# Gated linear attention feeding four experts: a state of two heads in 96 columns, and the additions and splits around it moved

## The chip, the cores and the metric

The kernel runs on one core of a Trainium2 chip. The metric is device time in microseconds (us) for one execution of the whole program. The core has a matrix engine (TensorE, called PE in the profile, with its weight loads listed apart as PEld), a vector engine (VectorE, DVE), a scalar engine (ScalarE, ACT), GpSimd (POOL) and a sync engine (SP) whose queue issues most of the transfers. Each engine works through its own instruction queue in order. Matrix products land in PSUM; everything else lives in SBUF or in device memory.

## The reference

Two blocks follow each other. The first is a gated linear attention over 4 batches, 8 heads, 768 positions and 48 features, with a state of 48x48 for each head:

```
state = alpha[:, :, t, :, None] * state + einsum('bhd,bhe->bhde', k[:, :, t], v[:, :, t])
y[:, :, t] = einsum('bhd,bhde->bhe', q[:, :, t], state)
```

Its result is laid out as 3072 rows of 384 (8 heads x 48). The second block sends every row through four experts and adds the results, weighted by normalised probabilities:

```
p = domain_probs / (domain_probs.sum(-1, keepdims=True) + 1e-09)
for e in range(4):
    h = np.maximum(x @ w1[e], 0.0)          # w1[e]: 384 x 1024
    out += p[:, e:e + 1] * (h @ w2[e])      # w2[e]: 1024 x 384
```

All is float32 on the outside.

## The kernel before

**Units and groups.** The 3072 rows are 24 units of 128 rows: 6 blocks of positions (`cb`) of each of 4 batches (`b`). The units are put in 7 groups: two units in the first (group 0) and the last (group 6), four in each of the five between. While the experts work on one group, the attention of the next group is woven in. `deal` makes a plan for that: each attention is a generator with some 17 steps, each step has a due time on a clock of estimated costs, and `advance` runs the steps that are due each time the expert loops add their estimated cost to the clock. What the plan yields is a fixed order of instructions for each engine.

**Experts.** For each group and each of the 4 experts there is an "up" stage (`up`, x @ w1, 8 column tiles of 128) and a "down" stage (`down`, h @ w2). From group 1 on, the up products are made from three parts of each float32 number: x is split into `top` (a rounded copy, made by ACT), `low` and `dif` (made by DVE, lines 242 and 243), and three fast float32r products (line 500) are summed, two parts into the PSUM tile `one`, the third into `two`. In groups 2 to 5 the down stage is made so too (line 576, `split2`). There the down stage goes over the four units in two turns of two ("pairs" below). A pair has 48 matmuls of 128x384: steps 0 to 23 are parts 0 and 1 of both units for the first six of the eight row tiles of h, steps 24 to 31 are the same parts for the last two row tiles (28 and 29 end part 1 of the first unit, 30 and 31 of the second), steps 32 to 39 are part 2 of the first unit, steps 40 to 47 part 2 of the second. Parts 0 and 1 are summed in the tile `ops0` of a unit, part 2 in `ops1`.

**Additions.** `add_up` (line 598) adds one such sum, scaled, to the unit's accumulator `acc`. In the kernel before, a unit's fine sum (`ops0`, scaled by `p_fine`) is added as soon as its part 1 is done, that is after step 29 for the first unit and after step 31 for the second; the other sum (`ops1`, scaled by `p_all`) after steps 39 and 47. With expert 0 the fine addition is a copy on ACT (line 607); all others are on DVE (line 609).

**The four banks.** `one`, `two`, `ops0` and `ops1` share four PSUM banks under the tag "g". A new tile takes the bank that comes free first in the program's order, and its first matmul waits until the last reader of the tile before is done. So the first matmul of the next pair, or of the next up stage, waits for the first fine addition of the pair before it.

**The second halves of `dif`.** The part `dif` of h is made by DVE in halves (line 542). The second halves are kept in a list, `later`, and one is issued at every fifth step of the down stages (steps 4, 9, 14, ..., 34, 39, 44).

**The next group's x.** `split_x` (line 450) makes the three parts of x for the next group during the last expert's down stage. In the kernel before, its step 0 makes `top` for all three column blocks of x in three ACT instructions (line 456) at the start of that stage; its steps 1 to 3 make `low` and `dif` of one column block each with two DVE instructions (lines 242 and 243), at 0.52, 0.62 and 0.72 of the stage. In groups 2 to 4 the two DVE instructions of a block have 128x512 elements, in group 5 128x256 (the last group has two units only).

**Attention.** Within a unit, scores are formed in seven levels of halving (lines 295 to 341); then line 415 makes the unit's output `yps` in three blocks `c` of 128 columns of PSUM partitions. Two heads make a pair `p`, four pairs in all. A head's 48 features are cut in 32 (`QUAD`) and 16 (`TAIL`): blocks 0 and 1 hold the first 32 features of four heads each, block 2 the last 16 of all eight heads. Four matmuls with 32 output columns each, side by side in the array, are a "turn" in this document. A turn reads either the state (`past`, against QT) or the values of this block of positions (against `lat`). The state `st` has 64 columns for a head: `sts` is 128 x 4 pairs x 2 heads x 64. In a pair the second head's last features lie in columns 48 to 63 and the first head's in columns 32 to 47, so that block 2 takes two turns on the state, one for each head of the pairs, and two on the values. After the output, line 436 makes keys^T with values for the pair in 128 columns (`sps`), and lines 442 to 445 decay the state and add to it (DVE, 64 partitions x 256 elements). That happens in 20 of the 24 units; 20 units read a state.

Of the kernel before, what the change touches and what calls it, by code (L numbers as in the profile page):

```python
# [20 lines left out]
def kernel(  # L21
# [37 lines left out]
    nc = tc.nc  # L59
# [45 lines left out]
    sts = [const.tile([P, NP, 2, HD], F32, name=f"st{b}") for b in range(B)]  # L105
# [48 lines left out]
    def load(u, names):  # L154
        if u >= len(units):
            return
        cb, b = units[u]
        for nm in names:
            src = srcs[nm][b, :, cb * P:(cb + 1) * P, :].rearrange("h s d -> s h d")
            if nm != "v":  # L160
                nc.sync.dma_start(out=raw(u, nm)[:, :, :D], in_=src)
                continue

            pairs = raw(u, nm).rearrange("p (a i) d -> p a i d", i=2)
            src = src.rearrange("p (a i) d -> p a i d", i=2)
            nc.sync.dma_start(out=pairs[:, :, 0, :D], in_=src[:, :, 0])
            nc.sync.dma_start(out=pairs[:, :, 1, :QUAD], in_=src[:, :, 1, :QUAD])
            nc.sync.dma_start(out=pairs[:, :, 1, D:], in_=src[:, :, 1, QUAD:])
# [70 lines left out]
    def split_rest(x, out):  # L239

        top, low, dif = out
        nc.vector.tensor_sub(low, x, top.bitcast(F32))  # L242
        nc.vector.scalar_tensor_tensor(out=dif, in0=top.bitcast(F32), scalar=1 / 4096.0,
                                       in1=low.bitcast(F32), op0=ALU.mult, op1=ALU.subtract)
# [18 lines left out]
    def attention(u):  # L263
# [140 lines left out]
        st = sts[b]  # L404
        yps = ps.tile([P, KC, P], F32, name="yps", tag="w")
        for c in range(KC):

            if c < 2:
                turns = [[(j, 2 * c + j // 2, j % 2, slice(0, QUAD)) for j in range(4)]]
            else:  # L410
                turns = [[(p, p, i, slice(QUAD, HD)) for p in range(NP)] for i in range(2)]
            terms = [(t, past) for past in ((True, False) if cb > 0 else (False,)) for t in turns]
            for n, (turn, past) in enumerate(terms):
                for j, p, i, cols in turn:
                    nc.tensor.matmul(  # L415
                        yps[QUAD * j:QUAD * (j + 1), c, :],
                        lhsT=st[:, p, i, cols] if past else rv[:, 2 * p + i, cols],
                        rhs=QT[:, p, :] if past else lat[:, 2 * p + i, :],
                        start=(n == 0), stop=(n == len(terms) - 1))
# [10 lines left out]
        if cb < NCB - 1:  # L430
            KB = AT
            nc.scalar.copy(out=KB, in_=turned(lambda p: KT[:, p, :]))
            yield
            sps = ps.tile([P, NP, 2, HD], F32, name="sps", tag="w")
            for p in range(NP):
                nc.tensor.matmul(sps[:, p], lhsT=KB[:, p, :], rhs=rv[:, 2 * p:2 * p + 2, :],  # L436
                                 start=True, stop=True)
            for i in range(2):
                rows = slice(HD * i, HD * (i + 1))
                old, add = st[rows, :, i, :], sps[rows, :, i, :]  # L440
                if cb == 0:
                    nc.vector.tensor_copy(out=old, in_=add)
                else:
                    nc.vector.tensor_mul(old, old, decs[-1][rows].broadcast_to([HD, NP, HD]))
                    nc.vector.tensor_add(old, old, add)
# [4 lines left out]
    def split_x(gi, step):  # L450

        n = len(groups[gi]) * P
        if step == 0:
            xTs[gi] = work.tile([P, 3, KC, NT], F32R, name="xT", bufs=1)
            for kc in range(KC):
                nc.scalar.activation(out=xTs[gi][:, 0, kc, :n], in_=xraws[gi][:, kc, :n],
                                     func=ACT.Copy, scale=TRIM)
        else:
            kc = step - 1
            split_rest(xraws[gi][:, kc, :n], [xTs[gi][:, part, kc, :n] for part in range(3)])  # L460
# [88 lines left out]
    def down(gi, e, slots, between):  # L549
# [14 lines left out]
        for n, (part, i, fc) in enumerate(steps):  # L564
# [17 lines left out]
            if part >= 1 and fc == FCH - 1:  # L582
                add_up(gi, e, slots[i], part // 2, sums[i][part // 2 if halves_ else 0])
        while between:
            between.popleft()[1]()
# [12 lines left out]
    def add_up(gi, e, slot, kind, part):  # L598

        cb, b = groups[gi][slot]  # L600
        at = b * NCB + cb
        if e == 0 and (kind == 0 or not split2(gi, e)):
            accs[cb, b] = hid.tile([P, DM], F32, name="acc", bufs=B)
        acc = accs[cb, b]
        scale = (p_fine if kind == 0 else p_all)[:, at, e:e + 1]
        if e == 0 and (kind == 0 or not split2(gi, e)):
            nc.scalar.activation(out=acc, in_=part, func=ACT.Copy, scale=scale)
        else:
            nc.vector.scalar_tensor_tensor(out=acc, in0=part, scalar=scale, in1=acc,  # L609
                                           op0=ALU.mult, op1=ALU.add)  # L610
        if kind == 0:
            return
# [50 lines left out]
    with tc.manual_schedule():  # L663
# [48 lines left out]
        for gi, e in ((gi, e) for gi in range(len(groups)) for e in range(E)):  # L712
# [6 lines left out]
            for k, slots in enumerate(turns):  # L719

                between = deque()
                if e == E - 1 and gi + 1 < len(groups):
                    for step, at in enumerate((0.0, 0.52, 0.62, 0.72)):
                        at = at * len(turns) - k
                        if 0 <= at < 1:
                            between.append((at, lambda step=step: split_x(gi + 1, step)))
# [33 lines left out]
```

## Time and profile before

| | |
|---|---|
| three runs | 1087.1 us median (1086.73 to 1088.61) |
| the profiled execution's own time | 1087.1 us |
| span of the profile in it | 1085.3 us |
| PE busy, PEld busy | 1062.9 us (98%), 892.9 us (82%) |
| DVE busy | 747.7 us (69%) |
| ACT busy | 560.7 us (52%) |
| POOL busy | 35.3 us (3%) |

The span is the profiled part of the execution; 1.8 us lie around it. In the page's 40 slices PE is at nine tenths or more from the sixth slice to the last but one. DVE is at six to eight tenths in most of them, and at one tenth in the last three. The first expert matmul (line 492) starts at 26.4 us, and the first one of group 1 (line 500) at 170.6 us. A line of a timeline merges instructions of one kind that follow each other: the first number is the start in us from the span's start, the second how long they took together, "x4" that they are four; brackets say how long the engine was idle before and what ended it. The last instruction's end can overlap the next one's start by some hundredths of a microsecond.

### The profile page before, as it was taken

The numbers are of one execution on the slowest core, as the hardware profiler recorded it, in microseconds if no ns is written. First come the engines' busy times: TensorE is split into PE (matmuls) and PEld (weight loads), VectorE is DVE, ScalarE is ACT, GpSimd is POOL, SyncE is SP. The second block draws the span as 40 slices with busy tenths as digits, with TensorE's granted clock in tenths as the row PEclk, the third lists the DMA queues.
The fourth block names the chain that finished last, engine by engine and source line by source line (L and its number), as shares of the span: only waits on it lengthen the run. The fifth ranks groups of instructions, "written<-read, shape, count | busy, mean of one in ns | idle before, by whom it ended". The sixth has DMA issues, their size and how long they took to land.

```text
span 1085.3 us, 21700 instructions
## 1 busy us (share of the span) xinstructions
PE 1062.9 (98%) x8532; PEld 892.9 (82%) x8532; DVE 747.7 (69%) x1625; ACT 560.7 (52%) x1191; POOL 35.3 (3%) x75
## 2 busy tenths in 40 slices
PE   8889899999999999999999999999999999999998
PEld 8767677686776798898898898898988998899876
DVE  5588678647557869778878787986786876757111
ACT  5787776674646555545546445555454454222321
POOL 2000000000000100000000000000000000000000
PEclk9999999999999999999999999999999999999999
DMA  8597789786696967657759559477477568545982
GB/s 124 154 327 216 228 266 370 290 312 234 211 322 218 400 203 275 273 169 301 254 171 358 201 190 357 158 276 306 151 291 287 201 259 349 235 197 238 309 312 91
DMA packets 166197, 273.68 MB, mean 252 GB/s; under 512 B 120624, under 2 KB 140976, under 8 KB 142032
## 3 DMA queue, kind: packets, MB, share of 16 engines
q1 hardware_dynamic: 156704, 230.06, 61.0%
q0 software_dynamic: 6016, 42.08, 9.9%
q8 instruction: 67, 1.10, 0.4%
q10 hardware_dynamic: 3376, 0.17, 0.3%
q14 instruction: 34, 0.28, 0.1%
HBM read 229.81 MB, written 42.47 MB: 251 GB/s over the span
## 4 chain that ended last, share of the span: by engine, by line
PE 87%; ACT 5%; DVE 5%; issue 2%; POOL 0%; ACTq 0%; DVEq 0%; POOLq 0%
PE ops L576 24%; PE one L500 21%; PE ops L580 13%; PE two L500 10%; PE sc L328 6%; PE yps L415 4%; PE one L492 3%; PE tp L260 3%; ACT qb L302 2%; PE sps L436 1%; PE far L383 1%; PE idle L689 1%; DVE near L338 1%; DVE hT L534 1%; DVE t L509 1%
## 5 line engine op out<-in xcount | busy, mean ns | idle before, releaser
L576 PE MATMUL ops<-w,hT 128*128 128x384 f32 x1536 | 284.7, 340 | 2.1 <-DVE acc L609 2.1
L500 PE MATMUL one<-xT,w 128*128 128x512 f32 (+1 forms) x1104 | 275.3, 385 | 0.8 <-DVE xT L242 0.8
L576 PEld LDWEIGHTS ops<-w,hT 128*128 128x128 f32 x1536 | 265.9, 188 | 5.7 <-DVE acc L609 2.8
L500 PEld LDWEIGHTS one<-xT,w 128*128 128x128 f32 x1104 | 194.5, 188 | 43.4 <-issue 2.6
L507 ACT ACTIVATE t<-one 128x512 f32<-128x512 f32 (+1 forms) x184 | 103.1, 560 | 149.4 <-PE one L500 148.8
L580 PE MATMUL ops<-hT 128*128 128x384 f32 x512 | 176.1, 491 | 0.0
L302 ACT COPY qb<-QT 64x256 f32<-64x256 f32 x336 | 136.5, 406 | 70.1 <-DVE QT L283 40.2
L500 PE MATMUL two<-xT,w 128*128 128x512 f32 (+1 forms) x552 | 148.3, 377 | 0.0
L580 PEld LDWEIGHTS ops<-hT 128*128 128x128 f32 x512 | 94.0, 191 | 56.5 <-issue 1.3
L534 DVE SCALAR_TENSOR_TENSOR hT<-t,hT 128x512 fp32r<-128x512 f32 x128 | 88.7, 693 | 61.1 <-ACT hT L532 59.7
L532 ACT ACTIVATE hT<-t 128x512 fp32r<-128x512 f32 x128 | 80.9, 632 | 95.8 <-DVE t L509 94.6
L500 PEld LDWEIGHTS two<-xT,w 128*128 128x128 f32 x552 | 100.3, 188 | 19.8
L542 DVE SCALAR_TENSOR_TENSOR hT<-hT 128x256 fp32r<-128x256 f32 x256 | 101.3, 421 | 4.4
L509 DVE TENSOR_TENSOR t<-t,two 128x512 f32<-128x512 f32 x128 | 87.3, 682 | 20.6 <-PE two L500 12.6
L609 DVE SCALAR_TENSOR_TENSOR acc<-ops,p_all,acc 128x384 f32<-128x384 f32 x88 | 53.3, 612 | 58.6 <-PE ops L580 42.3
L338 DVE COPY_PREDICATED near<-masks,sc 128x256 f32<-128x256 uint8 x144 | 77.0, 535 | 17.6 <-PE sc L328 14.5
L309 DVE TENSOR_TENSOR QT<-QT,dec 128x256 f32<-128x256 f32 x144 | 60.7, 421 | 32.5 <-ACT qb L302 32.0
L328 PEld LDWEIGHTS sc<-qb,KT 128*64 128x64 f32 x2304 | 72.5, 138 | 8.9 <-issue 6.3
L512 DVE TENSOR_TENSOR hT<-t,two 128x512 f32<-128x512 f32 (+1 forms) x56 | 32.1, 574 | 65.8 <-ACT t L507 56.1
L328 PE MATMUL sc<-qb,KT 128*64 128x64 f32 x2304 | 76.7, 223 | 0.3 <-ACT qb L302 0.3
L321 DVE TENSOR_TENSOR KT<-KT,dec 128x256 f32<-128x256 f32 x144 | 60.1, 417 | 2.2 <-PE tp L260 2.2
L320 ACT COPY KT<-KT 128x256 f32<-128x256 f32 x144 | 59.8, 415 | 3.1
(79 smaller groups left out, 927.0 us busy)
## 6 DMA issues: line engine op xcount, KB each, us to landing
w<-kept SPq DMA_DIRECT2D x156, 1152.0 KB
kept<-w POOLq DMA_DIRECT2D x32, 1152.0 KB, 7.5
hT<-in_moe_w_dram SPq DMA_DIRECT2D x48, 384.0 KB
w<-in_moe_w_dram SPq DMA_DIRECT2D x60, 128.0 KB
ra<-in_alpha_dram SPq DMA_DIRECT2D x23, 192.0 KB
rk<-in_k_dram SPq DMA_DIRECT2D x23, 192.0 KB
rq<-in_q_dram SPq DMA_DIRECT2D x23, 192.0 KB
out_dram<-acc POOLq DMA_DIRECT2D x22, 192.0 KB, 5.8
```

The source lines that it names most:

```text
L302: nc.scalar.copy(out=qb[rows, :, i, :].rearrange("p a (b r) -> p a b r", r=m), in_=qv[rows])
L309: nc.vector.tensor_mul(qv, qv, spread(dv[:, :, :, 0], m))
L328: nc.tensor.matmul(out[HALF * s:HALF * (s + 1), 2 * p:2 * p + 2, :], lhsT=KTs[li][:, p, HALF * s:HALF * (s + 1)], rhs=qbs[li][:, p, :, QUA ...
L338: nc.vector.copy_predicated(near.rearrange("p a (b two r) -> p a b two r", two=2, r=m)[:, :, :, 1, :], mk.unsqueeze(1).broadcast_to([P, H, ...
L500: nc.tensor.matmul(out, lhsT=w[:, part, kc], rhs=xTs[gi][:, part, kc, :n], start=(part == terms[0] and kc == 0), stop=(part == terms[-1] a ...
L507: nc.scalar.activation(out=t, in_=one, func=ACT.Copy, scale=FINE)
L509: nc.vector.tensor_add(t, t, two)
L532: nc.scalar.activation(out=top, in_=x, func=ACT.Relu, scale=TRIM)
L534: nc.vector.scalar_tensor_tensor(out=low, in0=x, scalar=0.0, in1=top.bitcast(F32), op0=ALU.max, op1=ALU.subtract)
L542: nc.vector.scalar_tensor_tensor(out=dif, in0=top.bitcast(F32), scalar=1 / 4096.0, in1=low.bitcast(F32), op0=ALU.mult, op1=ALU.subtract)
L576: nc.tensor.matmul(sums[i][part // 2], lhsT=h[:, part], rhs=w, start=(fc == 0 and part != 1), stop=(fc == FCH - 1 and part != 0))
L580: nc.tensor.matmul(sums[i][0], lhsT=h[:, 2].bitcast(F32), rhs=w, start=(fc == 0), stop=(fc == FCH - 1))
```

## The change

Three things change together.

- **The state and what is read of it.** The state of a pair of heads takes 96 columns in place of 128: first head's 32 features, first head's last 16, second head's last 16, second head's 32. The last features of both heads lie side by side in columns 32 to 63, and block 2 reads them in one turn. `sps` has 96 columns, and the DVE instructions of the state have 64 x 192 elements. The values are laid out to match: of the second head the last 16 features come first. The values themselves keep 64 columns for a head, with zeros behind the features, and block 2 still takes two turns on them.
- **The additions of a down stage.** A unit's two sums are added together after its part 2: `ops0` and then `ops1` of the first unit after step 39, of the second after step 47.
- **The split of the next group's x.** One column block at a time, `top` on ACT and then `low` and `dif` on DVE, at 0.25, 0.5 and 0.75 of the last expert's down stage. With two pairs this is step 24 of the first pair, step 0 of the second and step 24 of the second.

```
-    sts = [const.tile([P, NP, 2, HD], F32, name=f"st{b}") for b in range(B)]
+    sts = [const.tile([P, NP, 2, D], F32, name=f"st{b}") for b in range(B)]
...
-            nc.sync.dma_start(out=pairs[:, :, 1, :QUAD], in_=src[:, :, 1, :QUAD])
-            nc.sync.dma_start(out=pairs[:, :, 1, D:], in_=src[:, :, 1, QUAD:])
+            nc.sync.dma_start(out=pairs[:, :, 1, :TAIL], in_=src[:, :, 1, QUAD:])
+            nc.sync.dma_start(out=pairs[:, :, 1, TAIL:D], in_=src[:, :, 1, :QUAD])
...
-    def split_rest(x, out):
+    def split(x, out):
         top, low, dif = out
+        nc.scalar.activation(out=top, in_=x, func=ACT.Copy, scale=TRIM)
         nc.vector.tensor_sub(low, x, top.bitcast(F32))
...
+        flat_st = st.rearrange("p a i d -> p a (i d)")
+        flat_v = rv.rearrange("p (a i) d -> p a (i d)", i=2)
...
             if c < 2:
-                turns = [[(j, 2 * c + j // 2, j % 2, slice(0, QUAD)) for j in range(4)]]
+                now = [[(2 * c + j // 2, j % 2, (0, HD + TAIL)[j % 2], 2 * QUAD * (j % 2))
+                        for j in range(4)]]
+                turns = ([(True, now[0])] if cb > 0 else []) + [(False, now[0])]
             else:
-                turns = [[(p, p, i, slice(QUAD, HD)) for p in range(NP)] for i in range(2)]
-            terms = [(t, past) for past in ((True, False) if cb > 0 else (False,)) for t in turns]
+                turns = [(True, [(p, 0, 0, QUAD) for p in range(NP)])] if cb > 0 else []
+                turns += [(False, [(p, i, QUAD + TAIL * i, 0) for p in range(NP)]) for i in range(2)]
...
-            sps = ps.tile([P, NP, 2, HD], F32, name="sps", tag="w")
+            sps = ps.tile([P, NP, 2, D], F32, name="sps", tag="w")
             for p in range(NP):
-                nc.tensor.matmul(sps[:, p], lhsT=KB[:, p, :], rhs=rv[:, 2 * p:2 * p + 2, :],
+                nc.tensor.matmul(sps[:, p], lhsT=KB[:, p, :], rhs=rv[:, 2 * p:2 * p + 2, :D],
                                  start=True, stop=True)
...
-    def split_x(gi, step):
+    def split_x(gi, which):
         n = len(groups[gi]) * P
-        if step == 0:
+        if 0 in which:
             xTs[gi] = work.tile([P, 3, KC, NT], F32R, name="xT", bufs=1)
-            for kc in range(KC):
-                nc.scalar.activation(out=xTs[gi][:, 0, kc, :n], in_=xraws[gi][:, kc, :n],
-                                     func=ACT.Copy, scale=TRIM)
-        else:
-            kc = step - 1
-            split_rest(xraws[gi][:, kc, :n], [xTs[gi][:, part, kc, :n] for part in range(3)])
+        for kc in which:
+            split(xraws[gi][:, kc, :n], [xTs[gi][:, part, kc, :n] for part in range(3)])
...
-            if part >= 1 and fc == FCH - 1:
-                add_up(gi, e, slots[i], part // 2, sums[i][part // 2 if halves_ else 0])
-        while between:
-            between.popleft()[1]()
+            if part >= 2 and fc == FCH - 1:
+                add_up(gi, e, slots[i], sums[i])
         background()
...
+        scales = (p_fine, p_all) if split2(gi, e) else (p_all,)
+        if e == 0:
             accs[cb, b] = hid.tile([P, DM], F32, name="acc", bufs=B)
         acc = accs[cb, b]
+        for j, (part, scale) in enumerate(zip(sums, scales)):
+            if e == 0 and j == 0:
+                nc.scalar.activation(out=acc, in_=part, func=ACT.Copy, scale=scale[:, at, e:e + 1])
+            else:
+                nc.vector.scalar_tensor_tensor(out=acc, in0=part, scalar=scale[:, at, e:e + 1],
+                                               in1=acc, op0=ALU.mult, op1=ALU.add)
...
-                    for step, at in enumerate((0.0, 0.52, 0.62, 0.72)):
-                        at = at * len(turns) - k
+                    for kc in range(KC):
+                        at = (kc + 1) / (KC + 1) * len(turns) - k
                         if 0 <= at < 1:
-                            between.append((at, lambda step=step: split_x(gi + 1, step)))
+                            between.append((at, lambda kc=kc: split_x(gi + 1, [kc])))
```

## The prediction

> **What bounds the kernel now.** I read the page's busy times and chain of waits, then the groups of instructions with shapes kept apart, then the timelines of DVE and PE at the ends of the down pairs.
>
> ```profile
> PE 1062.9 (98%) x8532; PEld 892.9 (82%) x8532; DVE 747.7 (69%) x1625; ACT 560.7 (52%) x1191; POOL 35.3 (3%) x75
> PE 87%; ACT 5%; DVE 5%; issue 2%; POOL 0%; ACTq 0%; DVEq 0%; POOLq 0%
> ```
>
> PE is the chain: PE work that goes after the first 142 us is gained, and a wait that PE gets is lost. Prices are in the groups (busy us, mean ns | idle before); a float32 matmul has two records, a float32r one has one:
>
> ```profile
> L576 PE MATMUL ops<-w,hT 128*128 128x384 f32 x1536 | 284.7, 340 | 2.1 <-DVE acc L609 2.1
> L436 PE MATMUL sps<-rv,AT 128*128 128x128 f32 x160 | 21.3, 276 | 1.3 <-ACT AT L432 1.3
> L436 PEld LDWEIGHTS sps<-rv,AT 128*128 128x128 f32 x160 | 20.7, 191 | 3.9 <-ACT AT L432 1.8
> L415 PEld LDWEIGHTS yps<-QT,st 128*32 128x32 f32 x640 | 17.5, 111 | 7.3 <-issue 6.5 <-ACT hT L532 0.7
> ```
>
> PE waits for an addition in only two places of line 576, 2.1 us in all. Both end the first pair of a last expert. This is DVE around the first, then PE there and at the second (start, duration, instruction):
>
> ```profile
> 514.42 1.42 DVE L542 SCALAR_TENSOR_TENSOR hT<-hT 128x256 fp32r<-128x256 f32 x4
> 515.76 1.13 DVE L609 SCALAR_TENSOR_TENSOR acc<-ops,p_fine,acc 128x384 f32<-128x384 f32 x2
> 516.81 0.41 DVE L309 TENSOR_TENSOR QT<-QT,dec 128x256 f32<-128x256 f32 x1
> 517.14 0.16 DVE L311 TENSOR_TENSOR dec<-dec 128x8 f32<-128x8 f32 x1
> 517.22 0.42 DVE L321 TENSOR_TENSOR KT<-KT,dec 128x256 f32<-128x256 f32 x1
> 517.56 0.75 DVE L542 SCALAR_TENSOR_TENSOR hT<-hT 128x256 fp32r<-128x256 f32 x2
> 518.23 0.61 DVE L609 SCALAR_TENSOR_TENSOR acc<-ops,p_all,acc 128x384 f32<-128x384 f32 x1
> ...
> 520.33 0.68 DVE L242 TENSOR_TENSOR xT<-x_raw,xT 128x512 fp32r<-128x512 f32 x1
> 521.04 0.69 DVE L243 SCALAR_TENSOR_TENSOR xT<-xT 128x512 fp32r<-128x512 f32 x1
> ```
>
> ```profile
> 514.19 1.12 PE L576 MATMUL ops<-w,hT 128*128 128x384 f32 x5
> 516.42 0.78 PE L576 MATMUL ops<-w,hT 128*128 128x384 f32 x3 [1.11 <-DVE acc L609]
> 686.15 1.13 PE L576 MATMUL ops<-w,hT 128*128 128x384 f32 x5 [1.01 <-DVE acc L609]
> ```
>
> The pair's matmuls are spaced 0.17 us, so it ends at 515.14. DVE is behind by then: it reaches the first fine addition only at 515.76, ends it at 516.36, and PE goes on at 516.42. PE's delay is 1.28 us (the bracket counts less, since the last matmul's tail overlaps it).
>
> **State read in one turn.** It takes one of four turns of block 2 from 20 units. In PE's timeline two such turns start at 362.82 and the next work at 363.26, so a turn is 0.22 us: 20 x 0.22 = **4.4 us gained**. PE is the bound in every unit that reads a state.
>
> **sps in 96 columns.** 21.3 us over 20 units is 1.065 us for eight records; with the last one's 276 ns that leaves 113 ns from one to the next. If the step goes with the columns, 96 take 85 ns: 160 x 28 ns = 4.5 us. But each record loads 128 columns of weights, and loads take 191 ns for 128 columns and 111 for 32: 0.83 ns a column, 107 ns for 128. Then only 6 ns x 160 = 1.0 us can go, and perhaps nothing. No row with 128-column weights here is spaced closer than 109 ns, so I take the load: **0.5 us gained**, ends 0 and 4.5. A loss has no reason: nothing is added.
>
> The Trainium skill, page "TensorE: Matmul & The Clock Gate", section "LDWEIGHTS (loading the stationary operand)", has a load take its columns divided by 1.2, in ns; by it 128 columns are 107 ns, and narrowing the moving side buys next to nothing. Going by the matmul row alone the total below would be 4 us lower, by the rule it stands.
>
> **State instructions of DVE.** 72 instructions of 64x256 become 64x192. 256 elements take 419 ns (line 445) and 512 take 682 (line 509), so 64 fewer save 66 ns, 4.7 us of DVE in all. Nearly all falls where DVE catches up anyway, before it waits 0.7 us for the last relu of an up stage (line 532); I count 0.2 us, ends 0 and 1.
>
> **Values.** Transfers, bytes and queue order stay as they were, but for two pieces of 32 and 16 features that swap; no wait in the list of waits is for them. Nothing. GpSimd zeroes less before the first transposes: nothing.
>
> **Additions later.** Each first fine addition moves from step 29 to step 39 on DVE, behind everything issued between: two halves of `dif` (steps 34 and 39), what attention has there, and in a last expert the first split of x (step 24). The next pair's first matmul waits for that addition. Its seventh takes the bank of the first unit's other sum, whose addition follows 0.53 us behind; the seventh comes 1.04 us after the first, so it waits for nothing more. For the place shown (515.1), the changed program's DVE order puts these ahead of the fine addition: the QT, dec and KT row (516.81 to 517.56, 0.75), the two halves (517.56 to 518.23, 0.67) and one split (520.33 to 521.65, 1.32): **2.74 us**. PE already waits for it, so all of it is lost: the delay grows from 1.28 to 4.02. The same at 685.0: another 2.74. The other pair ends, where DVE has slack or not (start of the fine addition against the pair's end, plus what is put ahead of it, plus 0.61 for itself and 0.06 to PE):
>
> ```profile
> 848.07 0.75 DVE L542 SCALAR_TENSOR_TENSOR hT<-hT 128x256 fp32r<-128x256 f32 x2
> 848.74 1.13 DVE L609 SCALAR_TENSOR_TENSOR acc<-ops,p_fine,acc 128x384 f32<-128x384 f32 x2
> 849.79 0.75 DVE L542 SCALAR_TENSOR_TENSOR hT<-hT 128x256 fp32r<-128x256 f32 x2
> 850.46 1.13 DVE L609 SCALAR_TENSOR_TENSOR acc<-ops,p_all,acc 128x384 f32<-128x384 f32 x2
> ```
>
> This pair ends at 849.47, so -0.73 + 0.67 (halves) + 1.32 (split) + 0.67 = 1.92 us of new wait. At 601.4 and 771.1: -0.79 + 1.07 (two halves, QT, dec) + 0.67 = 0.95, less 0.09 waited today: 0.86 each. At 642.5: -1.04 + 0.67 + 0.67 = 0.30. At 925.7: -0.78 + 0.67 + 0.67 = 0.56. At 996.1, where the split has 256 columns: -1.22 + 0.67 + 0.79 + 0.67 = 0.91. At 433.4, 474.4, 811.3 and 960.5 the fine addition starts 1.8 to 2.8 us before the end: none (0.7 to 1.3 us are put ahead). With expert 0 it is on ACT, which idles there: none. Second pairs end with DVE less loaded: none. At 527 and 697 PE waits 0.14 us today for a sum behind the splits, which then goes: 0.28 gained. Sum: 5.48 + 1.92 + 1.72 + 0.30 + 0.56 + 0.91 - 0.28 = **10.6 us lost**; ends 7.4 (the three last experts alone) and 13.
>
> **Splits later.** The 18 instructions for `top` stay on ACT, spread out. ACT's idle time covers them (0.8 us before 513.3, 2.2 before 517.3, 4.3 before 354.8); at 515.1 the first would end near 513.1, and DVE reaches the matching `low` 2 us later. Without that cover DVE waits, at most 0.6 us for each. At the end of group 1's down stage (357.4) the last split moves behind a weight split (two times 0.95 us) and ends about when PE wants it: 0 to 0.6 us lost, I take 0.2.
>
> **The clock.** One PE wait of today is nearly that long, 3.5 us for `lat` before 123.17. After it the window's granted clock (last but two columns) is:
>
> ```profile
> 122.00:127.00 5.00, 3.83 (x58) 3.14 (x59) 2.63 (x8) 3.23 (x8) 0.53 (x1) 0.66 0.74 291
> ```
>
> 0.34 x 5 us = 1.7 us lost. Waits of 3.1 us (80.9) did nothing. Two waits of 4.0 us can cost 0 to 3.4; I take one, **1.7 us lost**. The same page's "Part 1: The HAM clock gate" asks for a whole idle window of 3.4 us on a free-running count; a wait of 4.0 us holds one in 18% of phases, which would make 0.6 of the 1.7.
>
> **Sum.** -4.4 - 0.5 - 0.2 + 10.6 + 0.2 + 1.7 = +7.4. The profiled execution took 1087.1 us, the median itself: 1087.1 + 7.4 = **1094.5 us**.
>
> **Rivals.**
> *The additions cost nothing, faster.* DVE's lag at a pair's end isn't carried over: it reaches the fine addition before PE needs it, in one place, the eight ends above. That most of the 32 pair ends have no wait today speaks for it; the rows of 515 and 686, where PE waits for that very addition, against. The gains alone: 1087.1 - 5.1 - 0.3 = 1081.7. It decides from where the new waits stay under 5.4 us in all.
> *Narrow `sps` pays in full.* 4.0 more gained: 1090.5. For it: steps of other matmuls go with columns. Against: the load row.
> *DVE's lag feeds on.* Both long waits halve the clock (+1.7) and the lag of the last experts also holds the up stage behind them, by an addition and a half split each time (some 1 us, four times): 1100.2. Against: a longer PE wait gives DVE that time back.
> *The change doesn't do what it says.* A turn less saves PE nothing because the next work waits: 1098.9. Against: the turns follow each other with no idle time (0.0 in that group).
>
> **How the numbers follow.** Forecast 0.66, its own range 1090.5 to 1098 (7.4 and 13 of waits, clock 0 to 3.4); faster rival 0.14; full `sps` 0.10; the last two 0.10. A measurement here tells some 0.2% (2.2 us) from no change. Within that lie the lower edges of forecast and `sps` case: 0.05. Slower 0.81, faster 0.14. The range leaves out the faster rival and little above: 1088 to 1100.2.
>
> **What would show it.** Right: PE idle before line 576's successor for the addition rises from 2.1 to near 12 us, in single waits near 4 us at two pair ends; yps from the state has 480 records in place of 640; the records of `sps` stay near 110 ns apart. Wrong: no such wait, or `sps` steps near 85 ns, or a first group of up matmuls waiting for xT.

## The result, and the profile after

The changed kernel takes 1098.4 us (median of four runs, 1096.9 to 1098.9) against 1087.0 (median of four runs, 1086.7 to 1088.6). The ratio is **1.0099, with a 95% interval of 1.0082 to 1.0117**: about 11 us slower. The forecast was 1094.5, its range 1088.0 to 1100.2. The profiled execution took 1096.9 us, with a span of 1095.1 us, 9.8 us longer than the 1085.3 before.

The page of the changed kernel, first its busy times and then the shares of its chain of waits:

```profile
PE 1063.9 (97%) x8372; PEld 892.0 (81%) x8372; DVE 746.9 (68%) x1625; ACT 561.5 (51%) x1191; POOL 34.9 (3%) x75
PE 74%; DVE 13%; ACT 7%; issue 3%; DMA 3%; SPq 1%; ACTq 0%; DVEq 0%
```

PE has 160 records fewer and yet 1 us more of busy time, in a span 10 us longer. DVE's share of the chain goes from 5% to 13%, though DVE itself has 0.8 us less to do. The groups of instructions, shapes kept apart (busy us, mean ns of one | idle before, and what ended it), show what was gained and where that went:

```profile
L422 PE MATMUL yps<-QT,st 128*32 128x128 f32 x480 | 24.6, 277 | 0.0
L444 PE MATMUL sps<-rv,AT 128*128 128x96 f32 x160 | 20.8, 273 | 1.3 <-ACT AT L440 1.3
L444 PEld LDWEIGHTS sps<-rv,AT 128*128 128x128 f32 x160 | 20.7, 191 | 3.9 <-ACT AT L440 1.8
L579 PE MATMUL ops<-w,hT 128*128 128x384 f32 x1536 | 289.6, 343 | 10.7 <-DVE acc L610 10.7
```

The reads of the state were, before:

```profile
L415 PE MATMUL yps<-QT,st 128*32 128x128 f32 x640 | 29.5, 280 | 0.0
```

They fall from 640 records to 480 and from 29.5 us to 24.6. `sps` falls from 21.3 us to 20.8, and its weight loads not at all. Against that stands the last row above: PE now idles 10.7 us before the down matmuls, all of it for an addition, where it was 2.1, and the matmuls themselves take 5 us more.

The two timelines around the first pair of group 2's last expert, DVE first, then PE there and at four later pair ends (start, duration, instruction; in brackets the idle time before and what ended it):

```profile
513.50 0.68 DVE L244 TENSOR_TENSOR xT<-x_raw,xT 128x512 fp32r<-128x512 f32 x1
514.22 0.69 DVE L245 SCALAR_TENSOR_TENSOR xT<-xT 128x512 fp32r<-128x512 f32 x1
514.83 0.75 DVE L545 SCALAR_TENSOR_TENSOR hT<-hT 128x256 fp32r<-128x256 f32 x2
515.50 0.42 DVE L311 TENSOR_TENSOR QT<-QT,dec 128x256 f32<-128x256 f32 x1
515.83 0.16 DVE L313 TENSOR_TENSOR dec<-dec 128x8 f32<-128x8 f32 x1
515.91 0.42 DVE L323 TENSOR_TENSOR KT<-KT,dec 128x256 f32<-128x256 f32 x1
516.25 0.75 DVE L545 SCALAR_TENSOR_TENSOR hT<-hT 128x256 fp32r<-128x256 f32 x2
516.92 0.61 DVE L610 SCALAR_TENSOR_TENSOR acc<-ops,p_fine,acc 128x384 f32<-128x384 f32 x1
517.64 0.62 DVE L610 SCALAR_TENSOR_TENSOR acc<-ops,p_all,acc 128x384 f32<-128x384 f32 x1
```

```profile
512.98 1.12 PE L579 MATMUL ops<-w,hT 128*128 128x384 f32 x5
517.58 1.20 PE L579 MATMUL ops<-w,hT 128*128 128x384 f32 x3 [3.48 <-DVE acc L610]
...
603.90 0.79 PE L579 MATMUL ops<-w,hT 128*128 128x384 f32 x3 [0.30 <-DVE acc L610]
...
691.01 1.28 PE L579 MATMUL ops<-w,hT 128*128 128x384 f32 x5 [3.46 <-DVE acc L610]
...
857.18 1.15 PE L579 MATMUL ops<-w,hT 128*128 128x384 f32 x5 [1.84 <-DVE acc L610]
...
1005.69 1.49 PE L579 MATMUL ops<-w,hT 128*128 128x384 f32 x7 [0.70 <-DVE acc L610]
```

The pair's matmuls end at about 513.9. DVE has then just begun the split of x, and still has to make four halves of `dif` and the QT, dec and KT row before it reaches the fine addition at 516.92. PE goes on at 517.58. Measured from the matmul spacing of 0.17 us, as the prediction did, the delay is 3.65 us here, 3.62 at 691.0, 2.00 at 857.2, 0.55 at 603.9, 0.56 at 777.3, 0.73 at 934.2 and 0.87 at 1005.7: 12.0 us, against 1.28 + 1.18 = 2.5 before. That is **9.5 us of new waits**.

The windows behind the waits (window, length, busy us of PE, PEld, DVE, ACT and POOL, granted clock, DMA share, GB/s):

```profile
514.10:517.58 3.48, 0.00 (x0) 0.00 (x1) 3.39 (x10) 1.71 (x4) 0.00 (x0) 1.00 0.00 0
517.80:521.20 3.40, 3.40 (x12) 3.40 (x12) 3.23 (x7) 0.00 (x0) 0.89 (x2) 0.50 0.45 115
691.80:695.20 3.40, 3.40 (x12) 3.40 (x12) 3.23 (x6) 0.00 (x0) 1.08 (x2) 0.51 0.47 118
857.20:860.60 3.40, 3.40 (x65) 3.15 (x67) 3.22 (x6) 0.00 (x0) 1.08 (x2) 1.00 0.20 73
```

While PE waits, DVE is busy 3.39 of 3.48 us: the wait is DVE's backlog, not a transfer. After both long waits the granted clock is 0.5 for 3.4 us, and PE records 12 matmuls where some 20 fit at their spacing of 0.17 us; half of 3.4 us is 1.7 us lost. After the wait of 2.0 us the clock stays at 1.00. This execution has one more such stretch at 80.9, before any expert's down stage in three parts, which the execution profiled before did not have (last section).

These add up to the span: 4.4 (turns) and 0.2 (`sps`, by the steps between its records; see the part on the prediction) gained, 9.5 of waits, 3.3 of clock behind the two long ones and 1.7 at 80.9 lost, is +9.9, against +9.8. The median lies 1.5 us above the profiled execution: the three other executions had a mean granted clock of 0.991 or 0.992, this one 0.994, the one before 0.998. Where these three lost it wasn't profiled; a later execution of the same kernel that was profiled, with a clock of 0.992, has the same four stretches of half clock, one of them twice as long.

### The profile page after: what moved, and what is told of

The parts are those of the page before. It is cut to its first block, busy times and chain, and to the rows that moved or that the text cites. A ratio compares the mean times of both kernels' runs of the same rounds, so it can differ in the third digit from the quotient of the medians.

```text
span 1095.1 us, 21380 instructions
## 1 busy us (share of the span) xinstructions
PE 1063.9 (97%) x8372; PEld 892.0 (81%) x8372; DVE 746.9 (68%) x1625; ACT 561.5 (51%) x1191; POOL 34.9 (3%) x75
## 4 chain that ended last, share of the span: by engine, by line
PE 74%; DVE 13%; ACT 7%; issue 3%; DMA 3%; SPq 1%; ACTq 0%; DVEq 0%
PE ops L579 20%; PE one L503 17%; PE ops L583 13%; PE two L503 8%; PE sc L330 5%; PE yps L422 3%; PE one L495 3%; DVE hT L537 3%; DVE t L512 2%; PE tp L262 2%; DVE hT L545 2%; ACT qb L304 2%; ACT hT L535 2%; PE far L385 1%; DVE near L340 1%
## 5 line engine op out<-in xcount | busy, mean ns | idle before, releaser
L579 PE MATMUL ops<-w,hT 128*128 128x384 f32 x1536 | 289.6, 343 | 10.7 <-DVE acc L610 10.7
L579 PEld LDWEIGHTS ops<-w,hT 128*128 128x128 f32 x1536 | 269.4, 190 | 15.7 <-DVE acc L610 12.8
L535 ACT ACTIVATE hT<-t 128x512 fp32r<-128x512 f32 x128 | 80.9, 632 | 96.1 <-DVE t L512 94.7
```

Source lines behind the costliest of these rows:

```text
L535: nc.scalar.activation(out=top, in_=x, func=ACT.Relu, scale=TRIM)
L579: nc.tensor.matmul(sums[i][part // 2], lhsT=h[:, part], rhs=w, start=(fc == 0 and part != 1), stop=(fc == FCH - 1 and part != 0))
```

## The experiments

The theory: the state's new layout gains nearly 5 us; the late additions and the late splits together put DVE's backlog ahead of the addition that PE waits for, and the clock's half stretches come on top. The rivals: the state's layout is itself the cause; one of the two moves would do it alone; the half clock belongs to something else than the waits.

### The state alone

The changed state, values and `sps`, with the additions and the split of x as before:

```
-            if part >= 2 and fc == FCH - 1:
-                add_up(gi, e, slots[i], sums[i])
+            if part >= 1 and fc == FCH - 1:
+                add_up(gi, e, slots[i], part // 2, sums[i][part // 2 if halves_ else 0])
+        while between:
+            between.popleft()[1]()
...
-                    for kc in range(KC):
-                        at = (kc + 1) / (KC + 1) * len(turns) - k
+                    for step, at in enumerate((0.0, 0.52, 0.62, 0.72)):
+                        at = at * len(turns) - k
...
```

> The state in 96 columns read in one turn, with the additions and the split as they were before. If the loss comes from the additions and the split alone, this keeps the gain alone: 20 turns of 0.22 us and some 0.3 us of sps, 1087.0 - 4.6 = 1082.4 us, with the two waits for an addition at 1.3 and 1.2 us as before. If the new layout itself costs time somewhere, it is 1087 or more.

Measured: 1083.0 us against 1088.4 of the kernel before on the same chip; by the paired runs a ratio of **0.9958 (0.9945 to 0.9971)**, 4.6 us faster. The group of down matmuls, and PE at the first of the two waits:

```profile
L583 PE MATMUL ops<-w,hT 128*128 128x384 f32 x1536 | 284.6, 340 | 1.6 <-DVE acc L616 1.6
```

```profile
514.04 1.66 PE L583 MATMUL ops<-w,hT 128*128 128x384 f32 x8 [0.85 <-DVE acc L616]
```

The state's layout is a gain, so it isn't the cause. It also shortens both old waits, from 1.28 and 1.18 to 1.01 and 0.92: 0.26 us each, four DVE instructions of the state at 66 ns. No kernel of this study is faster.

### Early additions, late splits

The changed kernel with only the additions put back:

```
-            if part >= 2 and fc == FCH - 1:
-                add_up(gi, e, slots[i], sums[i])
+            if part >= 1 and fc == FCH - 1:
+                add_up(gi, e, slots[i], part // 2, sums[i][part // 2 if halves_ else 0])
...
```

> The changed kernel with the fine additions back at steps 29 and 31; the split of x stays late. By the theory that PE waits for whatever DVE has ahead of the first fine addition, one split of 1.32 us stands ahead of it at the first pair of each last expert: waits of 2.6, 2.5 and 1.3 us (groups 2, 3, 4) and 0.2 us (group 5), 4.1 us more than before. With the gain of 4.6 us: 1086.5 us, and no half clock after these waits. By the rival that the late split costs nothing: 1082.4 us.

Measured: 1088.8 us, ratio 1.0012 (1.0002 to 1.0023). PE at the first of the three waits, and the windows behind the first two:

```profile
515.07 3.26 PE L579 MATMUL ops<-w,hT 128*128 128x384 f32 x12 [2.07 <-DVE acc L610]
```

```profile
516.20:519.60 3.40, 3.40 (x13) 3.40 (x12) 3.37 (x8) 1.14 (x3) 0.78 (x2) 0.50 0.18 59
686.90:690.30 3.40, 3.40 (x13) 3.40 (x12) 3.37 (x10) 1.44 (x3) 0.54 (x1) 0.50 0.08 25
```

The waits are 2.23, 2.25 and 1.26 us, somewhat shorter than expected. But half clock follows the first two all the same, which the expectation excluded for waits of this length, and the kernel is slower for it. Against the state alone the late splits cost 0.54%, some 5.9 us: 3.8 of waits (5.74 less 1.93), which leaves 2.1 for the clock. The two stretches of the profiled execution would be 3.3; whether the other executions had both wasn't profiled.

### Late additions, early splits

The changed kernel with only the split of x put back:

```
-                    for kc in range(KC):
-                        at = (kc + 1) / (KC + 1) * len(turns) - k
+                    for step, at in enumerate((0.0, 0.52, 0.62, 0.72)):
+                        at = at * len(turns) - k
                         if 0 <= at < 1:
-                            between.append((at, lambda kc=kc: split_x(gi + 1, [kc])))
+                            between.append((at, lambda step=step: split_x(gi + 1, step)))
...
```

> The changed kernel with the split of x as before; the additions stay together after part 2. By the theory: 1.42 us more ahead of the addition at the first pair of the last experts of groups 2 and 3 (waits 2.7 and 2.6), 0.6 in group 4, 0.12 in group 5, 0.9 twice, 0.3 and 0.6 at the other experts: 6.1 us more than before, 1087.0 - 4.6 + 6.1 = 1088.5 us, and no half clock. By the rival that the two late moves cost only through each other: 1082.4 us.

Measured: 1091.4 us, ratio 1.0027 (1.0014 to 1.0040). PE at the first wait, and the window behind it:

```profile
517.64 2.23 PE L583 MATMUL ops<-w,hT 128*128 128x384 f32 x9 [2.18 <-DVE acc L616]
```

```profile
518.90:522.30 3.40, 3.40 (x13) 3.30 (x12) 3.26 (x8) 0.00 (x0) 0.79 (x2) 0.50 0.55 151
```

The waits are 2.34 at both long places and 0.56 to 0.73 at four others, below what was expected by 0.3 at most places. Again half clock follows both long ones. Neither move does it alone: against the state alone the late splits cost 0.54%, the late additions 0.69%, both together 1.41%, or 1.23% by the later run of the changed kernel (1.0081, below): the sum, as near as these intervals tell. In the waits this is plain: at the first pair of group 2 they are 1.01, 2.23, 2.34 and 3.65; the steps from the first, 1.22 and 1.33, make 2.55 of the 2.64.

### The waits filled

To tell the clock from the waits, the changed kernel was given 14 idle products on PE just ahead of the second pair at the two long waits. Their result isn't used:

```
+        if gi in (2, 3) and e == E - 1 and slots[0] > 0:
+            awake = ps.tile([P, P], F32, name="awake", tag="w")
+            for _ in range(14):
+                nc.tensor.matmul(awake, lhsT=ident, rhs=ident, start=True, stop=True)
         for n, (part, i, fc) in enumerate(steps):
```

> The changed kernel with 14 idle 128x128 matmuls (3.1 us of PE) put where PE waits 3.65 us at the last experts of groups 2 and 3. They add nothing to the wait itself. By the theory that the idle time halves the clock for 3.4 us afterwards, these two half clocks go and 3.4 us with them: 1095.0 us, PEclk 1.00 right after both waits. If the clock falls anyway, or costs nothing because DVE is behind there: 1098.4 us.

Measured: 1094.8 us, ratio 1.0062 (1.0049 to 1.0076) where the changed kernel has 1.0099 (1.0082 to 1.0117): 4.0 us gained, give or take 2.4, by adding work. PE at the first place, and the windows behind both:

```profile
511.82 1.12 PE L583 MATMUL ops<-w,hT 128*128 128x384 f32 x5
512.77 3.29 PE L570 MATMUL awake<-ident 128*128 128x128 f32 x28
516.43 2.35 PE L583 MATMUL ops<-w,hT 128*128 128x384 f32 x12 [0.37 <-DVE acc L614]
```

```profile
516.40:520.00 3.60, 3.57 (x22) 3.54 (x23) 3.37 (x6) 0.00 (x0) 0.84 (x2) 1.00 0.41 104
688.10:691.70 3.60, 3.52 (x22) 3.48 (x23) 3.35 (x7) 0.00 (x0) 0.79 (x2) 1.00 0.40 102
```

The second pair starts no earlier for the filling: its delay behind the first pair is what it was (516.43 less 511.82 is 4.61; 517.58 less 512.98 is 4.60). But it then runs 22 matmuls at full clock where the changed kernel ran 12 in nearly the same time. So the half clock is caused by PE being idle in the wait. From the one timeline to the other, 1.6 us are gained behind each wait: 3.2 of the 4.0.

### How much idle time halves the clock

After these runs I put the stretches of half clock in all nine profiled executions beside PE's idle time. Within an execution they all begin at multiples of 3.413 us from each other, and each begins where a stretch of this grid ends in which PE was idle for most of the time. So the theory became: the clock of a grid stretch is set by the idle share of the one before, and where a wait falls on the grid decides as much as its length. Three kernels on one chip test it: the filling of the fourth experiment with 8 products, with 3, and the changed kernel once more.

```
-            for _ in range(14):
+            for _ in range(8):
```

> The changed kernel with 8 idle products (the result isn't used) ahead of the second pair at the two long waits, in place of 14. Theory, read from the nine executions profiled so far: the granted clock is set for stretches of 3.413 us on a fixed grid, and a stretch is at half clock when PE was idle for about 58% or more (2.0 us) of the stretch before. 8 products take about 1.9 us of the 3.5 us of idle time and leave 1.6, so no phase of the grid gives a half stretch behind either wait: clock 1.00 there, and the gain of 14 products in full, ratio to before 1.006. Rival, that any PE wait of some 1.3 to 2 us can halve the clock, or that the array has to be busy up to the end of the wait: half clock behind one or both of the waits, ratio 1.008 to 1.010.

```
-            for _ in range(14):
+            for _ in range(3):
```

> The same with 3 products, which take 0.7 us and leave about 2.8 us of idle time. Theory of the grid: a grid stretch holds 2.0 us or more of a wait of 2.8 us in (2.8 - 0.58) / 3.413 = 65% of the phases, so in the profiled execution half clock follows a wait exactly where the grid stretch that the wait fills most holds 2.0 us of idle time; in time some two thirds of the stretches of no filling, ratio 1.007 to 1.010. Rival, that an idle stretch has to be idle as a whole: no half clock behind any wait of 2.8 us, ratio 1.006.

The changed kernel itself:

> The changed kernel once more, on the same chip and profiled once more, for the comparison with the two runs beside it. Theory of the grid: waits of 3.65 and 3.62 us, half clock behind each in about 90% of the phases (a wait of 3.65 holds 2.0 us of one grid stretch in nearly every phase); ratio 1.009 to 1.011; every half stretch of the execution on one grid of 3.413 us, and before each of them a grid stretch with 2.0 us or more of idle PE.

Measured on the same chip: 8 products 1093.9 us, ratio **1.0052** (1.0037 to 1.0067); 3 products 1097.3 us, 1.0078 (1.0059 to 1.0097); none 1097.7 us, 1.0081 (1.0062 to 1.0101). So 8 products gain as much as 14 did, within the intervals, and 3 gain nothing that can be measured. With 8 the idle time left is 1.7 us, and the clock stays full behind both waits:

```profile
516.50:519.91 3.41, 3.39 (x21) 3.35 (x22) 3.19 (x6) 0.00 (x0) 0.65 (x2) 1.00 0.39 102
688.30:691.71 3.41, 3.41 (x21) 3.38 (x22) 3.23 (x6) 0.00 (x0) 0.70 (x2) 1.00 0.40 104
```

With 3 products two waits of the same length are left, and only the first is followed by half clock (for two steps of the grid, to 525.1). PE at both, and the windows of the grid stretches that hold them and those that follow:

```profile
518.95 1.33 PE L583 MATMUL ops<-w,hT 128*128 128x384 f32 x3 [2.81 <-DVE acc L614]
...
693.53 0.79 PE L583 MATMUL ops<-w,hT 128*128 128x384 f32 x3 [2.83 <-DVE acc L614]
```

```profile
514.89:518.30 3.41, 1.24 (x10) 1.05 (x8) 3.38 (x11) 1.80 (x5) 0.00 (x0) 1.00 0.00 0
518.30:521.71 3.41, 2.76 (x9) 2.76 (x10) 3.16 (x7) 0.49 (x1) 0.54 (x1) 0.50 0.18 59
688.90:692.31 3.41, 1.80 (x14) 1.61 (x12) 3.38 (x10) 1.55 (x4) 0.00 (x0) 1.00 0.00 0
692.31:695.72 3.41, 2.19 (x13) 2.19 (x14) 3.26 (x7) 1.03 (x2) 0.54 (x1) 1.00 0.07 22
```

The first wait lies mostly in one grid stretch (PE busy 1.24 of 3.41 us), the second is cut in two by the grid (1.80 and 2.19 busy), and no half clock comes of it. So the theory of the grid holds, and both rivals fall: length alone doesn't decide, and a stretch need not be idle as a whole. The kernel of the last experiment below agrees: its two long waits, with 2.60 and 2.59 us of idle time (to 526.5 and 700.5), are cut by the grid, and its execution has no half clock there. The mark of 58% was too sharp, though. Behind the wait of 1.8 us at the first pair of group 4's last expert (856 to 858 and 851 to 853 us) a stretch of half clock came in this execution and in that with 8 products, with idle shares of 55% and 52%; the last section has the count. With none, the long waits are again followed by half clock, both of them; but the stretch that begins at 122.7 us there follows one with 56% (1.9 us) and lasts two steps, which that expectation, with 2.0 us before each, didn't allow.

### The halves moved out of the way

Of what stands ahead of the addition, four halves of `dif` can go. In the changed kernel they are issued at every third step of second pairs only, so that no first pair has any:

```
-            if later and n % 5 == 4:
+            if later and slots[0] > 0 and n % 3 == 2:
```

> The changed kernel with the second halves of dif (0.335 us each on DVE) taken out of the first pair of a down stage and made in the second pair (steps 2, 5, ..., 23) instead. Additions and split stay late. By the theory that the waits are DVE's lag, up to eight halves less ahead of the first fine addition take 2.0 to 2.7 us off each wait: 1.0 to 1.6 us stay at the last experts of groups 2 and 3, the others go, and with them the half clocks: some 4 to 6 us faster than before, 1083 us where before takes 1088. By the rival that the additions are too late by their place in the program, with the waits following the steps: as the changed kernel, 11 us slower than before.

Measured: 1086.4 us, ratio **0.9986 (0.9977 to 0.9994)**: 1.1%, some 12 us, faster than the changed kernel and slightly faster than the one before, though additions and splits stay late. It doesn't reach the state alone (0.9958). The waits for additions, us in total, times, longest, and PE at the first place and at the up stage behind it:

```profile
PE one L503 <- DVE acc L610: 2.4, 2, 1.2
...
PE ops L579 <- DVE acc L610: 1.6, 2, 0.8
```

```profile
514.34 0.97 PE L579 MATMUL ops<-w,hT 128*128 128x384 f32 x4 [0.81 <-DVE acc L610]
...
526.39 1.66 PE L503 MATMUL one<-xT,w 128*128 128x512 f32 x6 [1.22 <-DVE acc L610]
```

As expected, the long waits fall to 0.97 and 0.98 us, the five others vanish, and no half clock follows. The gain fell short of the 4 to 6 us expected against the kernel before, because the halves now load the second pair: its end is late, and the next up stage waits 1.39 and 1.36 us for it. The theory had looked at the first pair alone and not at all that DVE does in the last expert's down stage.

### The halves moved, with the state alone

The same line in the kernel with the state alone, whose two waits of 1.01 and 0.92 are the last ones left:

```
-            if later and n % 5 == 4:
+            if later and slots[0] > 0 and n % 3 == 2:
```

> The new state alone, with additions and split as before, and the second halves of dif moved to the second pair as well. By the theory both remaining waits (1.0 us each) go: 4.6 + 2.0 us faster than before, 0.6%, and 0.2% faster than the state alone. If the second pairs get late by the moved work, the gain is less than that of the state alone (0.42%).

Measured: 1084.5 us, ratio 0.9963 (0.9950 to 0.9976), no better than the 0.9958 (0.9945 to 0.9971) without that line: a miss. PE in the second pair, and the window of the whole down stage:

```profile
524.38 1.31 PE L583 MATMUL ops<-w,hT 128*128 128x384 f32 x6 [0.92 <-DVE hT L549]
```

```profile
505.00:527.00 22.00, 21.08 (x156) 20.05 (x153) 20.61 (x48) 8.74 (x20) 1.08 (x2) 1.00 0.36 103
```

The wait for the addition is gone, and in the second pair PE waits 1.09 us (and 0.99 in group 3) for the halves themselves. DVE is busy 20.6 of 22.0 us in that stage: PE's wait can be moved about in it, but as long as that stage keeps so much DVE work it doesn't go.

### What an `sps` matmul costs

The changed kernel with four more matmuls ahead of the `sps` of each unit, same weights, but only 32 moving columns. The real ones write over what these leave:

```
             for p in range(NP):
+                nc.tensor.matmul(sps[:, p, :, :QUAD // 2], lhsT=KB[:, p, :],
+                                 rhs=rv[:, 2 * p:2 * p + 2, :QUAD // 2], start=True, stop=True)
+            for p in range(NP):
                 nc.tensor.matmul(sps[:, p], lhsT=KB[:, p, :], rhs=rv[:, 2 * p:2 * p + 2, :D],
...
```

> The changed kernel with four more matmuls ahead of those of sps in every unit that makes it: the same 128 columns of weights, and 32 columns of values (two heads' first 16). They are overwritten by the real ones. If a record's spacing goes with the columns that are read, theirs is 28 ns and the 160 records cost 4.5 us; if it is bound by the load of 128 columns, theirs is 107 to 112 ns as with 96 and 128 columns, and they cost some 18 us.

Measured, in one execution: span 1104.4 us. The two groups:

```profile
L447 PE MATMUL sps<-rv,AT 128*128 128x96 f32 x160 | 22.2, 282 | 0.0
L444 PE MATMUL sps<-rv,AT 128*128 128x32 f32 x160 | 19.7, 267 | 1.3 <-ACT AT L440 1.3
```

From the second record of a unit on, one of 32 columns follows the one before at 112 ns, as those of 96 and of 128 columns do. The extra records cost 0.9 us a unit, 17.9 us over 20 units, where 18 were expected if the load of 128 weight columns sets the step and 4.5 if the moving columns did. So the moving columns don't. That it is the load, and not some other price of a record, is seen at the first record of a unit, whose weights are loaded ahead of it. So it is in the changed kernel too, weight loads first, then matmuls:

```profile
497.25 1.09 PEld L444 LDWEIGHTS sps<-rv,AT 128*128 128x128 f32 x8
497.48 1.02 PE L444 MATMUL sps<-rv,AT 128*128 128x96 f32 x8
```

There the step from the first record to the second does go with the moving columns: 109 ns with 128, 82 with 96, 28 or 29 with 32, in 17 of the 20 units of each kernel (in the three others, all before 155 us, it is 104 ns longer or 64).

## Why the prediction was right or wrong

The direction, the mechanism and its places were right; the time came out 3.9 us above the forecast, inside its range and just above the forecast's own range (1090.5 to 1098).

- **State read in one turn.** Right. 4.4 us were put; the timeline shows 0.20 to 0.22 us less in each up stage that holds such a turn, and the group is 4.9 us smaller. The experiment with the state alone has the whole layout at 4.6 us faster.
- **sps in 96 columns.** Right, and by the reason given; the size was put too high. 0.5 us were put, and the group's busy time is 0.5 smaller, but only half of that reaches the work behind. The first step of a unit gets 27 ns shorter (109 to 82), all others between its records stay at 112 ns. In 11 of the 20 units the step from the last record to the work behind grows by as much (31 to 58 ns), so that a unit's records take 807 ns as before; the nine others gain 27 ns each, 0.24 us in all. "Narrow `sps` pays in full" falls with the last experiment. The Trainium skill's page "TensorE: Matmul & The Clock Gate", section "LDWEIGHTS (loading the stationary operand)", divides the columns by 1.2 to get ns; the estimate of 107 ns that this makes for 128 columns is near the 112 that was measured at 32, 96 and 128 moving columns.
- **State instructions of DVE.** Undersized. They were put at 0.2 us, since DVE was taken to catch up where it waits 0.7 us for a relu. But four of them stand ahead of each of the two additions that PE already waited for, and those waits for the relu (506.46 and 509.00 before) stay 0.70 us long in the changed kernel too, so nothing is absorbed there: 0.26 us gained at each addition, 0.5 together, as the experiment with the state alone shows. The same step explains most of what the long waits fell short, 3.65 and 3.62 in place of 4.02.
- **Values.** No wait for them came up; nothing was put.
- **Additions later.** Right in kind and place. Of 10.9 us of new waits (10.6 net of the 0.28 at the up stages behind), 9.5 came. The two long waits are 0.4 below, mostly by the term just named; 1.92 at 857 came as 2.00, 0.91 at 1005.7 as 0.87, 0.56 at 934 as 0.73. The two of 0.95 came as 0.55 and 0.56, and of the 0.30 in group 2 nothing is seen: around that pair's end (645.1) PE's records stay 0.17 to 0.18 us apart. "The additions cost nothing" falls with the DVE and PE rows of 513.5 to 517.6. The working was complete in naming the split of x as part of what stands ahead. The two experiments with one move each show it: 2.34 us with the additions alone, 2.23 with the splits alone, 3.65 with both.
- **Splits later.** The `top` instructions cost nothing that could be seen: in the changed kernel ACT is idle half of the long wait. Of the bound of 0.6 us nothing was needed, and the 0.2 put for the end of group 1's down stage didn't come: PE has no wait for xT there.
- **The clock.** The term that was mis-sized. One of the two long waits was given a stretch of 1.7 us; in both executions of the changed kernel that were profiled both had one, 3.3 us, and filling the waits gave back 4.0 us by the first comparison and 3.2, give or take 2.7, by the second (1.0052 beside 1.0081). With 3.3 in place of 1.7 and 9.5 in place of 10.6 the same sum gives +7.9. What is missing to the median's +11.3 is 1.7 at 80.9 in the profiled execution, and 1.5 between that and the median, which goes with a lower mean clock there. The 1.7 at 80.9 isn't shown to be the change's doing: the idle time at that place is 2.7 us in the kernel before too, and half clock follows it in some executions and not in others. The later run of the same kernel was 1.0081, 8.8 us slower than before. There is some luck in how near the forecast came: the waits were put 1.1 us too high and the clock 1.6 too low, and the two errors hide each other. The belief behind the term, that a wait must be nearly 3.5 us long, was wrong: the experiments with one move each show half clock behind waits of 2.2 and 2.3 us. The 3.1 us at 80.9 which did nothing were counted from start to start; the row has 2.74 us of idle time, measured as the 3.50 of the other wait. Worked out from the runs, with 2.0 us of one grid stretch idle as the condition, a wait with 3.48 us of idle time meets it in (3.48 - 0.59) / 3.41 = 85% of the phases.
- **DVE's lag feeds on.** Its first half (both waits halve the clock) came, its second hardly: behind the last experts of groups 2 and 3 the next up stage (529.8, 703.2) starts with no wait for a sum. PE's long wait gives DVE time to catch up, as had been argued against it; that this is the reason wasn't tested.

## What to carry to other kernels

When an instruction is moved later on an in-order engine, list what is then ahead of it, and ask whether another engine waits for it at a place where the engine is already behind: there the whole list is lost, elsewhere only what exceeds the engine's lead. A gain of 4.6 us on the bounding engine was outweighed by moving work that takes no longer than before, and taking apart the three parts of the change was what found the good one. Where PE waits for some two microseconds or more, look at the granted clock after the wait: the price can be half as much again, and idle products in the wait gave that part back here.

## What the runs showed of the hardware

**The granted clock follows the idle share on a fixed grid.** In the twelve profiled executions of this study all stretches of half clock begin on a grid of 3.413 us, whose phase differs from one execution to the next, and last one step of it (three last two steps: those that begin at 122.7, 122.9 and 518.3). Those at the very end aside, I laid that grid over PE's records from 40 to 1075 us: some 3600 stretches at full clock. In 24 of them PE was idle for more than 58.6%, and half clock followed each of these. Between 50% and 58.6% are nine (eight without one that begins before 40 us), and it followed four of them. In all the others PE was idle for 50% or less, and it followed none. So half clock needs some 1.7 to 2.0 us of idle time within one grid stretch.

This is why one and the same wait costs 1.7 us in one execution and nothing in the next. At about 80 us, long before the first late addition or split, PE has an idle time of 2.7 us in each of these kernels. The stretch that holds it and the next one, first of the changed kernel, then of the kernel with the late splits:

```profile
77.47:80.88 3.41, 0.68 (x22) 0.58 (x25) 0.96 (x3) 3.31 (x8) 0.00 (x0) 1.00 0.77 276
80.88:84.29 3.41, 3.41 (x32) 1.95 (x23) 3.13 (x6) 3.07 (x8) 0.00 (x0) 0.50 0.32 114
```

```profile
79.30:82.71 3.41, 1.81 (x37) 1.50 (x38) 0.98 (x4) 3.34 (x9) 0.00 (x0) 1.00 0.50 173
82.71:86.12 3.41, 3.41 (x71) 2.64 (x69) 3.38 (x7) 2.36 (x7) 0.53 (x1) 1.00 0.30 104
```

In the first, PE is busy 0.68 us of the stretch, and 32 matmuls follow in 3.41 us; in the second 1.81 us, and 71 follow. The price can be read from the records of the first group's up products: from the first to the 101st it takes 77.7 us in the six executions of the new layout that have this stretch, and 76.1 in the four without it (the kernel with additional `sps` matmuls aside), 1.6 us less. The Trainium skill's page "TensorE: Matmul & The Clock Gate", section "Part 1: The HAM clock gate", has a free-running window of 3413 ns, and the runs agree to the nanosecond or two. It also has the slow state come after an idle window; read as a window idle throughout, the runs differ, since one idle for 60% was enough each time. What decides between 50% and 59% was not found, nor why three stretches lasted two steps.

**A floor for matmuls with 128 float32 weight columns.** Their records follow each other at 112 ns with 32, 96 and 128 moving columns alike, except for the first of a row, whose weights are loaded before it.
